# Two PSUM banks for the corrections u, and another order of the work, in a linear-attention and gated-convolution kernel on one core

## The chip, the core and the metric

The kernel runs on one core of a Trainium2 chip. The metric is the device time of one execution in microseconds; the time before is the median of three runs. Engines are named as in the profile: PE is TensorE (PEld its weight loads), DVE is VectorE, ACT is ScalarE, POOL is GpSimd, SP is SyncE, which issues most of the transfers.

## What is computed

Two parts, one after the other: a recurrent attention with decay and delta rule, whose output is the input of a network with a short convolution and a gate. B = 4, H = 8, S = 768 and D = 40; the network goes from 320 to 1024 features and back.

```
state = zeros((B, H, D, D))
for t in range(S):
    y[:, :, t] = einsum('bhd,bhde->bhe', rt, state)
    Sa = einsum('bhde,bhe->bhd', state, at)
    state = state * wt[:, :, None, :] - einsum('bhd,bhe->bhde', Sa, bt)
    state = state + einsum('bhd,bhe->bhde', vt, kt)
x = y.transpose(0, 2, 1, 3).reshape(B, S, H * D)
h = maximum(x @ w_in, 0)
conv = sum(conv_w[k] * shifted(h, k) for k in range(3))
out = (h * 1 / (1 + exp(-conv))) @ w_out
```

## The kernel before

The 768 tokens are cut into 24 steps of 32 tokens. Two steps are a pair (12 of them), prepared together; two steps of output are also a window of 64 tokens (12), the unit of the network.

For each pair, the loads w, a, k and b arrive by SP's queue; `decays` makes running products of the decays on VectorE, `decayed` multiplies them in and turns the results (products pa, pk and pb). `scores` makes the products ps for each step. `solve_in` and `solve` invert a small triangular system by 31 rounds of two operations (a multiplication, L566, and an addition, L572), on VectorE for even pairs and on GpSimd for odd ones, and bring the result `tt` into place through DRAM.

For each step, `chain` is the part that hangs on the step before: the products pp, from the state (L598) and from the values and scores (L608), are copied with a minus sign to `psb` by ScalarE; pu (L624) multiplies that by `tt` and gives u, the corrections; four evictions write u into `vu` beside the values (L631 to L638: ScalarE has the quadrants 1 and 2, VectorE 0 and 3); pn (L649) makes the state's addition from vu and the hatted keys kb; VectorE adds it, GpSimd scales the new state (L664). Beside the chain stand the turns of values, state and r (pv L673, pt, pr), the products pm (L717) and their masking ms, from_state (py L741), outputs (py L755), and `finish`, which turns the output (pq L776), scales it into xf (VectorE, L781) and splits it into xh and xl (ScalarE L789, GpSimd L791). `pack` copies parts of xh to xp and xl by three transfers on SP's queue. `moe_in` is the first projection, 16 products ph (L816) for each quarter of the features, of which the seventh reads xp, then the convolution, the gate and their evictions; `moe_out` is the second projection, po (L863).

The products ps, pm, pn, pp (two parts), pu and py (two parts) come as groups of 64 small products, of 32 or 40 columns each; the others are 3 to 16 larger ones. In what follows a run is a sequence of such small groups with no larger product between.

PSUM holds three tiles of two banks each (pp, pu, pn, ps and the others by `banks`) and two of one bank (ph and po). Though pu is a two-bank tile, its products use bank 0 alone.

The order is written out by hand. Each part of the work is a generator; the string ORDER names, one after another, which one advances to its next `yield` (`ch8*3`: the chain of step 8, three advances; we pieces of weights, ld lv lr loads, de decays, dd decayed, sc scores, si and so the solver, ch chain, vt st rt turns, fs from_state, pa pairs, ou outputs, fi finish, pk pack, mi and mo the two projections, mi3.1 being window 3 and quarter 1). `emit_all` (L926) walks it under `tc.manual_schedule()`, so each engine executes its instructions in the sequence in which this text emits them.

Of the kernel before, what the change touches and what calls it, by code (L numbers as in the profile page):

```python
# [38 lines left out]
we11 we10 dd2 ld3 dd2 we10*3 we12 so0 dd2*2 so0*2 we12 so0*2 so1 we11 we12*3 so1 sc4*3 sc5 we11
sc5*2 we11*2 so1 ro0 we13 we14 ro0*2 ch0*2 so1 we13*2 vt0 ch0 vt0*2 pa0 ch0 we15 we14*2 lv2*2 ch0*2  # L40
so1 ch1 we16 ch1 si2*2 pa0*2 we15*2 ch1 ou0 ch1 ou0*2 fi0 ch1 st1 so1 st1*2 fi0 ch1 we16*2 fi0 we17
vt1 we18 fs1*2 lv3*2 vt1*2 fi0*2 ch1 pa1 so1 rt1 pa1*2 ou1 lr2*2 rt1*2 ha3 ou1*2 ch1*2 fi1 ha3*2
we17*2 ha4 so1 ha4*2 ch2 we19 ch2 st2 ch2 fi1 so1*2 de3 we18*2 fi1 st2*2 fi1*2 fs2*2 we19*2 de3*2
dd3 we20 we21 pk0*2 mi0.3*2 we20*2 ld3*2 we22 ld4 ch2 we21*2 mi0.3 mi0.2*2 mi0.3 ch2 mi0.2 we22*2
ch2 mi0.2 mi0.3 mi0.2 ch2 dd3*2 vt2 ch2*2 mi0.2 dd3*2 lv4*2 dd3 mi0.3 dd3 ld4 vt2*2 dd3 mi0.2 so2
dd3*2 ch3 mi0.3 ch3 pa2 ch3 mi0.2*2 ch3 pa2*2 mi0.0*2 ch3 ld4 ou2 so2 ch3 ou2*2 fi2 vt3 ch3 mi0.0
fi2 lv5*2 ch3*2 so2 sc6 fi2 mi0.0 ch4 vt3*2 fi2*2 ch4 sc6*2 mi0.0 so2 sc7 ch4 st3 ha5 st3*2 sc7*2
ha5*2 fs3*2 so2 si3*2 pa3 st4*3 pa3*2 mi0.0 rt2 ou3 rt2*2 mi0.3*2 lr3*2 ha6 ou3*2 so2 mi0.0 fi3
mi0.1*2 ha6*2 mi0.1 fi3 de4 so2 fi3 fs4*2 ld4*2 mi0.1*2 fi3*2 pk1*2 so2 de4*2 dd4 so2*2 so3*2 dd4*2
mi0.0*2 mi1.0 mi1.2 dd4*4 so3 dd4 mi0.1 dd4*2 mi1.0*2 ch4 so3 mi1.0 mi0.1 ch4 mi0.1*2 mi1.1 mi1.0  # L50
ch4 ld5 mi1.0 mi1.1 vt4 ld5 mi1.1 ch4 so3 lv6*2 mi1.1 mo0.1 vt4*2 mi1.0 sc8 ld5 mi1.1 mi1.0*2 pa4
sc8*2 mi1.2 ch4*2 mi1.1 sc9 so3 mi1.2 sc9*2 mo0.1 pa4*2 si4*2 mi1.2 mi1.1 ch5 mi1.2 mi1.1*2 ou4
mi1.2 ch5 so3 ou4*2 fi4 ch5 st5 fi4 ch5 fi4 st5*2 mo0.1 ch5 fi4*2 mo0.1 so3 ch5 mo0.1*2 vt5 ch5
so3*2 so4 ha7 ch5*2 vt5*2 fs5*2 ha7*2 pa5 ch6*2 mi1.3*2 ch6 pa5*2 so4 ou5 st6 ou5*2 fi5 st6*2 rt3
fi5 lv7*2 so4 fi5 de5 rt3*2 fi5*2 ha8 ch6 ha8*2 ld5*2 de5*2 ch6 dd5 lr4*2 mi1.3 mo0.0 pk2*2 mi1.3
mi1.2 mo0.0 mi1.3 mo0.0 ld6 dd5*2 ch6 so4 dd5*2 vt6 ld6 mo0.0 ch6 lv8*2 dd5*2 ch6*2 dd5 fs6*2 vt6*2
# [957 lines left out]
```

## Time and profile before

| | before |
|---|---|
| median of three runs | 720.21 us (718.52 to 724.62) |
| profiled execution | 721.62 us |
| its span, first to last instruction | 719.9 us |
| mean granted clock of TensorE | 0.844 |
| PE, DVE, ACT, POOL busy | 579.1, 466.2, 251.9, 229.8 us |
| moved by DMA | 65.47 MB |

Times are in microseconds from the start of the span. In a timeline a row gives start, duration, engine, line, operation, output and inputs with their tile names, shapes, the number of instructions in the row, and in brackets how long the engine was idle before and what released it; "issue" means that nothing in the profile was waited for. The granted clock is a share of full speed.

### The profile page before, as it was taken

How to read it: one execution, taken by the hardware profiler on the slowest of the kernel's cores; microseconds unless marked ns; L12 is line 12 of the kernel's file. 1: busy time of each engine (PE TensorE's matmuls, PEld its weight loads, DVE VectorE, ACT ScalarE, POOL GpSimd, SP SyncE). 2: the span in 40 equal slices, each digit the busy share in tenths (PEclk: the TensorE clock that was granted, in tenths of full speed). 3: DMA queues.
4: the chain of work that ended last, by engine and by line, in shares of the span. 5: the costliest groups of instructions: out<-in, count | busy, mean ns of one | idle time of the engine just before them, and what ended most of it. 6: DMA issues, size and time to landing. Idle time of an engine off the chain costs nothing.

```text
span 719.9 us, 31917 instructions
## 1 busy us (share of the span) xinstructions
PE 579.1 (80%) x14265; PEld 498.3 (69%) x14265; DVE 466.2 (65%) x1091; ACT 251.9 (35%) x553; POOL 229.8 (32%) x466
## 2 busy tenths in 40 slices
PE   2760179668777988889888989989889899888998
PEld 2650168558766777677677778878778788777884
DVE  8888978878974765613866736987435686432541
ACT  1110013233242334323424435434433345543551
POOL 6010187001582010555014840124650108701000
PEclk9975557878898978967988989989988899997999
DMA  9889845552662643925724835634733534120011
GB/s 158 154 152 153 134 127 120 128 103 41 116 123 50 110 96 70 152 43 81 148 45 80 139 76 89 115 69 92 139 54 69 115 60 77 19 40 22 18 31 29
DMA packets 260278, 65.47 MB, mean 91 GB/s; under 512 B 233428, under 2 KB 255980, under 8 KB 260140
## 3 DMA queue, kind: packets, MB, share of 16 engines
q1 hardware_dynamic: 249940, 59.37, 46.3%
q10 hardware_dynamic: 10200, 4.06, 2.8%
q8 instruction: 112, 1.84, 1.1%
q14 instruction: 26, 0.21, 0.1%
HBM read 38.63 MB, written 10.22 MB: 68 GB/s over the span
## 4 chain that ended last, share of the span: by engine, by line
PE 26%; issue 6%; DMA 5%; DVE 5%; POOL 4%; ACT 2%; SPq 2%; ACTq 1%; POOLq 0%; DVEq 0%
PE po L863 7%; PE ph L816 5%; DMA bb<-bd 2%; PE pm L717 2%; POOL xx L572 2%; POOL st L566 2%; PE pv L673 1%; DMA bd<-at 1%; PE ps L510 1%; PE pn L649 1%; PE pp L608 1%; PE pt L700 1%; PE py L755 1%; PE pp L598 1%; PE pu L624 1%
## 5 line engine op out<-in xcount | busy, mean ns | idle before, releaser
L863 PE MATMUL po<-wo,g 128*128 128x320 f32 x384 | 120.5, 460 | 5.4 <-ACT hb L830 3.5
L845 DVE SCALAR_TENSOR_TENSOR cc<-hb,cw,cc 128x256 f32<-128x256 f32 x192 | 89.3, 527 | 21.5 <-ACT cc L837 21.4
L566 POOL TENSOR_TENSOR st<-xx,bb 128x126 f32<-128x126 f32 (+22 forms) x186 | 72.4, 389 | 75.8 <-DMA bb<-bd 30.8
L863 PEld LDWEIGHTS po<-wo,g 128*128 128x128 f32 x384 | 73.5, 201 | 31.8 <-issue 5.6
L572 POOL TENSOR_TENSOR xx<-xx,st 128x126 f32<-128x126 f32 (+22 forms) x186 | 77.6, 417 | 14.6
L664 POOL TENSOR_TENSOR state<-state,a 104x640 f32<-104x640 f32 x23 | 34.0, 1478 | 141.1 <-DVE state L661 125.4
L791 POOL TENSOR_TENSOR xl<-xf,xh 120x384 fp32r<-120x384 f32 x24 | 24.5, 1021 | 135.4 <-ACT xh L789 135.4
L566 DVE TENSOR_TENSOR st<-xx,bb 128x126 f32<-128x126 f32 (+22 forms) x186 | 55.8, 300 | 13.8 <-DMA bb<-bd 8.2
L816 PE MATMUL ph<-xh,wih 120*128 120x256 f32 x288 | 63.0, 331 | 0.0
L830 ACT ACTIVATE hb<-ph 128x512 f32<-128x512 f32 x48 | 28.7, 598 | 88.6 <-PE ph L816 88.3
L572 DVE TENSOR_TENSOR xx<-xx,st 128x126 f32<-128x126 f32 (+22 forms) x186 | 52.6, 283 | 6.4
L635 DVE COPY vu<-pu 32x320 f32<-32x320 f32 x48 | 23.3, 486 | 46.9 <-ACT vu L637 46.9
L855 DVE TENSOR_TENSOR g<-cc,hb 128x512 f32<-128x512 f32 x48 | 33.8, 714 | 25.1 <-ACT cc L850 20.7
L816 PEld LDWEIGHTS ph<-xh,wih 120*128 120x128 f32 x288 | 46.2, 210 | 3.4 <-issue 0.8
L510 PE MATMUL ps<-a,k 40*64 40x32 f32 x1536 | 36.0, 246 | 10.5 <-issue 5.3
L837 ACT ACTIVATE cc<-hb,cw 128x256 f32<-128x256 f32 x96 | 43.2, 500 | 0.2
L510 PEld LDWEIGHTS ps<-a,k 40*64 40x64 f32 x1536 | 32.7, 165 | 15.1 <-issue 9.0
L816 PE MATMUL ph<-xl,wih 120*128 120x256 f32 x192 | 41.8, 302 | 0.0
L724 DVE TENSOR_TENSOR ms<-pm,tri 128x512 f32<-128x512 f32 x24 | 16.5, 687 | 36.0 <-PE pm L717 35.9
L781 DVE TENSOR_TENSOR xf<-pq,pre 120x384 f32<-120x384 f32 x24 | 13.3, 554 | 39.7 <-PE pq L776 37.1
L717 PE MATMUL pm<-r,v 40*64 40x32 f32 x1536 | 34.0, 240 | 6.0 <-issue 4.9
L608 PE MATMUL pp<-vu,at 32*32 32x40 f32 x1536 | 25.9, 222 | 15.4 <-issue 15.4
(306 smaller groups left out, 1191.5 us busy)
## 6 DMA issues: line engine op xcount, KB each, us to landing
bb<-bd SPq DMA_DIRECT2D x24, 256.0 KB
w<-in_w_dram SPq DMA_DIRECT2D x24, 160.0 KB
a<-in_a_dram SPq DMA_DIRECT2D x24, 160.0 KB
k<-in_k_dram SPq DMA_DIRECT2D x24, 160.0 KB
rin<-in_r_dram SPq DMA_DIRECT2D x24, 160.0 KB
vu<-in_v_dram SPq DMA_DIRECT2D x96, 40.0 KB
b<-in_b_dram SPq DMA_DIRECT2D x24, 160.0 KB
k<-kt SPq DMA_DIRECT2D x24, 160.0 KB
```

Of the source, the lines that this page charges most:

```text
L510: nc.tensor.matmul(ps[half(z), x, y * 128 + hp * C : y * 128 + hp * C + C], k64[half(x, D), 2 * y + c, kp, z], a64[half(x, D), c, y, hp, z ...
L566: eng.tensor_tensor(t3, xx[:, 0:nj, i : i + 1].to_broadcast([128, nj, nt]), bb[:, i : i + 1, i + 1 :].to_broadcast([128, nj, nt]), ALU.mult,)
L572: eng.tensor_tensor(xx[:, 0:nj, i + 1 :], xx[:, 0:nj, i + 1 :], t3, ALU.add)
L608: nc.tensor.matmul(pp[quad(bi), x, hp * D : hp * D + D], at[kv(bi), c, y, x, hp], vu[kv(bi), y, KEY[x][hp], 0:D], start=(first and hp == 0 ...
L664: nc.gpsimd.tensor_tensor(new, new, al[..., 0:1].to_broadcast([SR, 2, 8, D]), ALU.mult)
L717: nc.tensor.matmul(pm[half(z), x, y * 128 + i * C : y * 128 + i * C + C], v64[half(x, D), y, i, half(z)], r64[half(x, D), y, i, quad(2 * z ...
L816: nc.tensor.matmul(ph[:, j], l[:, fs], x, start=(j == 0 and i == 0), stop=(i == len(passes) - 1), skip_group_check=True,)
L830: nc.scalar.activation(out=hb[:, :, :, 2 : W + 2], in_=ph, func=AF.Relu)
L837: nc.scalar.activation(out=cc[:, j], in_=hb[:, j, :, 1 : W + 1], func=AF.Copy, scale=cw[:, 1, f : f + 1],)
L845: nc.vector.scalar_tensor_tensor(out=cc[:, j], in0=hb[:, j, :, x : W + x], scalar=cw[:, x, f : f + 1], in1=cc[:, j], op0=ALU.mult, op1=ALU ...
L855: nc.vector.tensor_tensor(g, cc, hb[:, :, :, 1 : W + 1], ALU.mult)
L863: nc.tensor.matmul(po[:rows, :DM], parts(f), wo[:, f, :], start=(f == 0), stop=(f == NF - 1))
```

## The change

The products pu of odd batches are written to bank 1 of their tile instead of bank 0, the even ones stay in bank 0. The quadrants 1 and 2 hold the even batches and 0 and 3 the odd ones, so ScalarE's two evictions now read bank 0 and VectorE's two read bank 1. No instruction is added. The text of ORDER is replaced as a whole: the same steps of the same generators in another sequence. The diff, with the order cut to a few lines (the old text has a run around `ch8` and one around `ch11`, the new one around `ch1`; the new text's other lines are around step 8 and the scores 13 to 15):

```diff
--- before.py
+++ after.py
@@ -31,90 +31,93 @@
 )
 
 ORDER = """
...
-ch7 mi2.0 fi6 ch7*2 so4 vt7 mi2.0 fi6 sc10 lv9*2 vt7*2 fi6*2 so4 mi2.0 ch8 st7*2 ch8 sc10*2 so4*2
-mi2.0 ch8 sc11 fs7*2 sc11*2 mi2.0 pa7 mi1.3 rt4 pa7*2 mi1.3 mi2.0*2 mi2.1 rt4*2 ou7 mi1.3*2 mi2.1
...
-ch10*2 pa10 sc14 pa10*2 mi3.3 mi3.1*2 ch11 sc14*2 ch11 so6 sc15 ch11 mo2.1 sc15*2 ch11 so6 mo2.1*2
-ou10 ch11 st11 ou10*2 si7*2 mi4.1*2 st11*2 mi4.1 so6 fi10 ch11 mi4.1*2 vt11 ch11 lv13*2 vt11*2 fi10
...
+we0*4 ld0 de0*2 ld0 dd0*2 ld0 we1 we2 ld0*2 dd0 ld1 dd0*5 de0 de1 we1 dd0 de1 sc0*3 sc1*2 ld1 we2
...
+pa0*2 we11 st1 ha2 lr0 st1 we11 rt0 dd2 sc4*3 sc5 dd2 so1 sc5 we10 we11 lr1 we10 pa0 we12 lv1 we12
...
+fi7*2 ld6 de6 dd6 mo2.1 dd6 ha9 sc11 pk3 ch8*3 mo2.1 mo2.0 lr5 ou7 ch8 fs8 pa7 ch8 dd6*3 ld6 dd6*4
+lv0 mi3.0 vt8 si5 ch8 mi3.0 ch8 vt8 so5*2 mi3.0 fs8 mo2.0 so5 pa8*2 mi3.1*2 mi3.0*3 so5 mi3.1*2 ch8
+so5*4 ch8 lv9 mi3.1 ld7 mi2.3 mo2.1 mi3.1 de6 ou8 mi3.0 ld7 fi7 sc12*3 sc13*2 mi3.0 mo2.1 ou8
...
+mi4.2 sc13 lv9 mi4.1 mi4.3 mo3.0 dd7 pa11 so6*2 ou11*2 fi10*2 lr5 dd7 mi4.2 sc14 fi11 mi4.2 mi4.1
+fi11*2 mi4.2 mi4.3 sc14*2 mi4.3 rt5 ha12 fi11 mi4.1 mi4.3 ha12 sc15*2 mi4.3 rt6*2 sc15 ld8 st12
...
@@ -622,15 +625,16 @@
             x, hp = KAT[h]
             for bi in range(B):
                 nc.tensor.matmul(
-                    pu[bu(bi), 0, h * D : h * D + D], pd["tt"][quad(bi), c, 4 * x + hp],
+                    pu[bu(bi), bi % 2, h * D : h * D + D], pd["tt"][quad(bi), c, 4 * x + hp],
                     psb[quad(bi), x, hp],
                     start=(h == 0), stop=True, skip_group_check=True,
                 )
         yield
 
         for i, q in enumerate((1, 0, 2, 3)):
-            dst = vu[quad(q), int(q in (0, 3)), :, 0:D]
-            src = pu[quad(q), 0, 0:HD].rearrange("p (h d) -> p h d", d=D)
+            y = int(q in (0, 3))
+            dst = vu[quad(q), y, :, 0:D]
+            src = pu[quad(q), y, 0:HD].rearrange("p (h d) -> p h d", d=D)
             if i % 2:
                 nc.vector.tensor_copy(dst, src)
             else:
```

## Rows read from the trace of the kernel before

**Rows 1.** the page: busy times, and three groups on GpSimd

```profile
PE 579.1 (80%) x14265; PEld 498.3 (69%) x14265; DVE 466.2 (65%) x1091; ACT 251.9 (35%) x553; POOL 229.8 (32%) x466
...
L566 POOL TENSOR_TENSOR st<-xx,bb 128x126 f32<-128x126 f32 (+22 forms) x186 | 72.4, 389 | 75.8 <-DMA bb<-bd 30.8
...
L572 POOL TENSOR_TENSOR xx<-xx,st 128x126 f32<-128x126 f32 (+22 forms) x186 | 77.6, 417 | 14.6
L664 POOL TENSOR_TENSOR state<-state,a 104x640 f32<-104x640 f32 x23 | 34.0, 1478 | 141.1 <-DVE state L661 125.4
```

**Rows 2.** five stages: stretch, length, PE PEld DVE ACT POOL busy, PE clock, DMA share, GB/s

```profile
0.00:126.00 126.00, 61.49 (x1437) 54.16 (x1438) 106.10 (x269) 20.06 (x41) 48.75 (x103) 0.72 0.83 143
126.00:216.00 90.00, 67.18 (x1832) 59.34 (x1832) 74.33 (x175) 30.57 (x66) 31.23 (x67) 0.81 0.52 102
216.00:432.00 216.00, 186.25 (x5040) 161.63 (x5040) 126.33 (x286) 78.03 (x167) 72.90 (x151) 0.83 0.52 91
432.00:666.00 234.00, 213.12 (x5517) 184.33 (x5516) 138.13 (x315) 100.89 (x223) 75.96 (x145) 0.90 0.40 74
666.00:720.00 54.00, 51.01 (x444) 38.85 (x442) 21.32 (x47) 22.34 (x59) 1.00 (x1) 1.00 0.11 26
```

**Rows 3.** waits of VectorE up to 216 us: total, times, longest

```profile
DVE vu L635 <- ACT vu L637: 8.6, 10, 2.8
```

**Rows 4.** timeline, one step's evictions of u: start, duration, operation

```profile
446.97 0.42 ACT L637 COPY vu<-pu 32x320 f32<-32x320 f32 x1 [0.28 <-PE pu L624]
...
448.41 0.42 ACT L637 COPY vu<-pu 32x320 f32<-32x320 f32 x1 [1.02 <-DVE vu L635]
...
448.86 0.50 DVE L635 COPY vu<-pu 32x320 f32<-32x320 f32 x1 [0.48 <-ACT vu L637]
```

**Rows 5.** waits of TensorE after 110 us: total, times, longest

```profile
PE pp L608 <- issue: 15.4, 8, 2.5
PE ph L816 <- DMA xp<-xh: 8.4, 2, 5.6
...
PE pn L649 <- DVE vu L635: 2.2, 3, 1.3
...
PE pn L649 <- issue: 1.0, 2, 0.8
...
PE pn L649 <- ACT vu L637: 0.7, 2, 0.5
```

**Rows 6.** TensorE's timeline in three places

```profile
318.14 1.93 PE L510 MATMUL ps<-a,k 40*64 40x32 f32 x114
321.32 0.43 PE L510 MATMUL ps<-a,k 40*64 40x32 f32 x14 [1.25 <-issue]
...
366.53 0.43 PE L863 MATMUL po<-wo,g 128*128 128x320 f32 x1
366.89 1.14 PE L717 MATMUL pm<-r,v 40*64 40x32 f32 x64
...
372.36 0.22 PE L608 MATMUL pp<-vu,at 32*32 32x40 f32 x1 [1.94 <-issue]
...
582.54 2.33 PE L863 MATMUL po<-wo,g 128*128 128x320 f32 x8
```

**Rows 7.** two stretches around the gap at 370 us, columns as stages

```profile
370.50:373.90 3.40, 1.54 (x66) 1.42 (x67) 1.98 (x8) 0.44 (x1) 0.00 (x0) 1.00 0.02 5
373.90:377.40 3.50, 3.50 (x101) 2.30 (x102) 2.74 (x9) 0.80 (x2) 0.00 (x0) 0.51 0.03 7
```

**Rows 8.** TensorE's timeline, product pn at either level of the clock

```profile
101.31 1.83 PE L649 MATMUL pn<-vu,kb 64*64 64x40 f32 x62
...
449.73 1.13 PE L649 MATMUL pn<-vu,kb 64*64 64x40 f32 x64
```

**Rows 9.** timeline around the second window's copies

```profile
182.46 0.55 DVE L781 TENSOR_TENSOR xf<-pq,pre 120x384 f32<-120x384 f32 x1
...
188.86 0.36 PE L816 MATMUL ph<-xp,wil 120*128 120x256 f32 x1 [2.80 <-DMA xp<-xh]
```

More of the change, by code (lines that the diff above doesn't have):

```diff
@@ L39 @@
[L39 to L56, printed above, removed]
@@ new lines @@
+we14 mi0.0 ch3 we17 st3 ha5*2 fi2*2 ch3 mi0.0 we18 ou2 mi0.2 we4 vt3 we11 st3 we17 lv4 we5 so2 vt3
+dd3 pa2 de3 fi2 dd3 fs3*2 pa3 we18 pa3 fi2 we19 rt1 ch3*2 ch4 lr2 ch4 fi2 ch4*2 we20 mi0.1 mi0.3
+sc5 dd3 lv5 rt2 ou3*2 rt2 we19 sc6 mi0.0 we20 sc6 mi0.1 mi0.0 mi0.3*2 we15 ch4 mi0.0 fi3 mi0.3 sc6
+sc7 we21 lv1 ou3 mi0.3 mi0.2 sc7 fi3 mi0.3 fi3 mi0.2 ha5 ld3 ld4*2 fi3 ch4*2 we21 vt3 st4 mi0.2*3
+vt4 st4 ld4 mi0.3 ha6 we7 we22*2 pk1 si3 de4 ha6 mi0.2*2 mi0.3 ld4 lv2 vt4*2 we10 ch4 mi0.0 mi1.0
+mo0.0 dd3 mo0.0 de4 fi3 mi1.0*2 fs4 ld4 ha6 we12 we21 dd4*2 sc7 mo0.0 mo0.1 mo0.0 fs4 de4 pa3 mi0.2
@@ new lines @@
+mi1.0 ld5 pa4 mi1.0 si3 ch4 pa4 dd4 lr3 dd4*3 we17 dd4*2 ou4 ha7 so2 mi0.3 ha7 so3*2 ou4 mi1.0*3
+ou4 ch5 mi1.2 ch5 so3*2 ch5 mi1.2*3 we22 mi1.0 dd4 ch5 we20 mi1.2 st4 mi1.3 ro0 pa4 fi4 st5 lv6 ch5
+mi1.2*2 ch5 fi4 ch5 mi1.3 mi1.2 mi1.3 lr3 st5 we18 mo0.0 mi1.3*2 so3 ha7 so3 vt5 dd4 ld5 vt5 sc8*3
+sc9 mi0.1 we8 sc9 mi1.3 mi1.1*5 mi1.3 fs5*2 pa5*3 ld5 si4 mo0.1 fi4 mi1.2 ou5 de5 mi1.1 ch5 ou5 fi4
+mi1.3 ld5 fi4 fi5*4 de5 so3 ch5 ch6*2 pk2 we16 mi1.1 mo0.0 mo0.1*2 dd5*2 st5 dd5 mo0.1 mi1.1 mo0.1
@@ new lines @@
+mo1.1 dd5 so3 ld5 mi1.1 so3 st6 so3 dd5 mo1.1 mi2.0*3 so4 mo1.1 fi5 mi2.0 lr2 st6 ch6 mi2.1 ou5
+mi2.1 dd5 mi2.1 dd5 rt2 mo1.1 so4*2 rt3 mo1.0*2 mi2.1 vt5 mi2.1 ld6 rt3 fs6 dd5*2 mi2.0 ch6 mi2.2
+mi2.1 mi2.0 mi2.1 pk2 ch6 mi2.1 mo1.1 so4 mi2.2 lv7 fs6 vt6*2 we12 mi2.2 ch6 pa6 ch6 mi2.2 mi1.3
+pa6 so4 ch6 mi2.3 lr4 ou6*2 mi2.0 st6 so4*2 sc9 vt6 mi2.1 so4 mi2.2 mo1.0 st7 ch6 fi6 ch7*2 ld6 st7
+ch7 mo1.0 st7 ha8*3 sc10*2 ch7*2 mi2.0 rt3 fi6 ou6 mi2.3*2 vt7 mi2.2 fi6*3 mi2.3 lv5 sc10 vt7 sc11
+ch7*3 ld6 mi2.3 de5 lv8 mi2.2 ch7 mi2.0 mo1.1 sc11 lv8 so4 ha9*2 si4 mi2.3 pa6 si5 mi2.2 dd5
@@ new lines @@
+ha11 so5 mi3.2 so5 so6 mi3.2 vt9 mi3.2 mo2.0 st9 fs9 fi8*2 fs9 pa9 mi3.3 pa9 mo3.1 mo3.0 ch9 lv6
+ch9 ch10 ou9 ch10 mi3.0 so6*2 ou9 fi9 mo3.1 ch10 ld7 fi9 st10*2 de7 pk0 so6 ou9 fi9*2 ch10*2
+mo3.1*2 pk4 ch10 mi4.0*3 lv11 ld7 rt5 dd6 so6 ch10 mi4.0 rt5 mi4.0 de7 mi4.2 st10 pa9 mi4.2 dd7 lr6
+ld7 mo3.1 ch10 mi3.1 dd7 mi4.0 ch10 si6 pk1 dd7 ch11*2 vt10*3 ch11 mi4.2 ld8 lv12 so6 dd7*3 ch11
+dd7 mo3.0 mi4.1 fs10*2 dd7 pa10 ch11 pa10*2 ch11 mi4.0 st11*2 mo3.0 ou10 ha11 so6 de7 ou10 mi4.0*2
+ch11 so6 fi9 mo3.1 ou10 fs11 vt11*2 ld8 mi4.1 fi10 mi4.1*2 vt11 fs11 pa11 mi4.2 fi10 st11 fi10 ch11
@@ new lines @@
+ch13 mi5.3 ld9*2 dd8 mo4.0 mo4.1 mi5.0*2 ha14 st13 mi5.0 ha14*2 st13 sc16*3 sc17 ch13*2 ou12 vt13
+mo4.0 fs13*2 vt13 sc17 mi5.3 st13 pa13*2 mi5.3*2 ha15 so7 ha15*2 mi5.3 ou13*2 de9 fi13 si8 ld9 so7
+fi13 mi5.2*2 mi5.3 fi13*2 sc17 de9 dd9*2 ou13 mi5.2 rt7 mo4.0 lr6 pk6 so7 mi5.2*3 rt7 ch13 de9
+mo4.0 dd9 vt13 ch13 pa13 ha16*2 mi5.2 so7 so8 ch14 st14 fi13 st14 mi6.0 dd9*3 mi5.2 so8 ch14 mi5.2
+fs14 ch14 mi5.1 mi6.0 pk3 lv12 dd9 mi6.1 dd9 mi6.0 ch14 mi6.2 ch14 mi5.3 mi6.0 st14 vt14 mi6.0 fs14
+lv15 mi6.0 vt14 ch14 pa14 ch14 so8 pa14 ch14 mi6.2 si8 lv11 mo4.0 mi6.2 mo4.0 ch14 ch15*2 so8 ch15
@@ new lines @@
+st15 ch15*2 mo5.0 st15 ch15 ha16 ou14*3 mi5.3 mi6.0 vt14 ld9 ld10*3 vt15 mi6.2*2 fi14 mo5.0 so8
+ch15 so8 mo4.1 vt15 ch15 lr8 fi14 pa14 fi14*2 mi6.0 so8*2 mo5.0*2 fi14 fs15*2 pa15 dd9 pa15 sc18
+mi6.1*2 vt15 lv14 ch15 sc18*2 mi6.2 lr7 mi6.3 st15 ou15 sc19*2 mi6.2 ou15 mo5.1 fi15 mi6.2 de10
+lv16 lv17 mo5.0 ch16*2 pk4 mi6.2 ch16 dd9 mi6.3*2 sc19 fi15 de10 dd10 mo5.1 so8 ch16 fi15 pa15 ou15
+fi15 mi6.1*3 ch16 mi6.1 dd10 st16 mo5.1 st16 ha17 mo5.1 si9 dd10 ld10 mo5.1 so8 ha17 rt7 mi6.0 ch16
+rt8 vt16 mi6.3 pk7 ld10 mi6.3 lr8 ch16 ha17 mi6.3 rt8 vt16 dd10*2 si9 ch16 so9 mi6.1 vt16 dd10 st16
@@ new lines @@
+ch16 fs16 mi6.3 lv18 ch17*2 mi6.3 ld11 fi15 fs16 so9*2 dd10 mi6.1 mi7.0 ch17 mi7.1*3 mi7.0*3 so9
+dd10 so9 mo5.1 mi7.0 dd10 lr9 mo6.1 ch17*2 mi7.1 pa16 ch17 pa16 mi7.1*2 ch17 st17*2 mo6.1 mi7.0
+ou16*3 fs17 pa16 mi7.2 ld11 vt17 fs17 lv19 lv16 mi7.1*2 vt17 mi7.1 mi7.2 ld11 mi7.2 so9 de10 sc20*3
+sc21*2 si10*2 mi7.0 ch17 mi7.0 st17 mi7.0 mi6.3 mi7.2*3 so9 fi16 mo6.1 mi7.3*3 fi16*3 ha18 pa17*2
+so9 ha18 mi7.3*3 ha18 sc21 mo5.0 mo6.1*2 rt8 ou17 rt9 ou17 fi16 fi17 de11 fi17 rt9 fi17 de11 fi17
+mo6.0*2 pk8 dd10 so9 dd11 mo6.0*2 ha19 dd11*2 mi7.3 so9 ou17 so10 ha19 st18 mi7.2 ch17 mi7.3 lr9
@@ new lines @@
+mo6.0 ha19 ha20 ch18*2 so10 ld11 mo6.1 mi7.2 ch18 mi8.1 mi8.0 mi8.1 mi8.0*2 mi8.1 mo6.0 st18 ch18
+so10 ha20 mo7.1*2 ch18 ha20 dd11 mi7.2 so10 vt17 mi7.3 ch18 dd11 ch18*2 dd11*3 mo7.1 ch18 pk6 so10
+mi8.0 vt18 fs18 mi8.0 vt18 lv20 so10 pa17 ch19*3 dd11 st18 mo7.0 mo7.1 fs18 ch19*2 pa18 mo7.1 mo7.0
+ha21 pa18 ou18 ld11 so10 mi8.3 so10 mo7.1 mi8.0 ou18 st19*2 sc22 ch19 ou18 sc22*2 sc23 mi8.0 so10
+ch19 pk7 mi8.0 st19 mi8.1 sc23 mi8.1*2 lv19 mi8.3*2 so10 ch19 vt18 vt19 ha21 mi8.3 vt19 mi8.1*2
+mi8.3 mo7.0 mi8.2 ha21 ch19 ch20*2 si11 pk5 fi17 ch20 fi18 ch20 mi8.2 ch20 fi18 mi8.2 fi18 mi8.3
@@ new lines @@
+ch20 st20 mo7.0 fi18 mi8.2 lv21 ch20 lr10 ch20 rt9 pa18 fs19*2 pa19 vt19 mi8.2 mo7.0 st20 mi8.2
+pa19 sc23 mi8.2 so11 mi8.3*2 pa19 st20 fi18 mi8.2 mo8.1 vt20 mi8.2 lv22*2 ch20 ou19 ch21 ou19 ch21
+vt20 fi19 ha22 fi19 mi8.1 fi19 so11 ha22 vt20 ou19 ch21 mo7.0 mi8.3 ha22 mo8.1*2 rt10 mi8.0 rt10
+fi19 so11 mo8.1 ch21 fs20 so11 fs20 ch21 so11 pk9 mi9.1*3 ch21*2 pk8 pa20*2 mo8.1 mi9.1*2 mo8.0
+ch21 st21 mi9.1 rt10 dd11 mo8.1 st21 vt21 lr11 mi9.1*2 ou20*3 fs21 so11 fs21 pa20 mi9.2*2 vt21 st21
+lv23 fi19 fi20 mi9.2 fi20*2 pk9 pa21 mi9.0*2 fi20 mi9.2*2 pa21 so11 lv20 lv23 fi20 mi9.0 ou21*2
@@ new lines @@
+mi9.2 rt11 mi9.2*2 rt11 mi9.3 fi21*4 mi9.2 vt21 mi9.0 so11 mi9.0*5 ch21 mi9.3*2 mo8.0 ou21 mo8.0*2
+st22 ha23 mi9.3*2 lr11 ha23 mi9.1 pk10 mi10.0 so11 st22 mi9.3 fi21 mi10.0*3 lv17 mi9.3 mi10.0*2
+mi9.3 pa21 mi10.0 ch22 fs22 ch22*2 rt11 mo8.0*2 mi10.2 mi10.1*3 ch22 mi10.0 ch22 mi10.2*2 vt22 fs22
+pk10 ch22*2 vt22 lv18 mi10.2 ch22*2 mi9.3 mi10.1 mi10.0 mi10.3 mo9.0 ha23 mi10.2*2 pa22 ch23*2
+mi10.1 si11 mi10.2*2 ch23 mi10.3 pa22 mi10.1 mi10.3 mo9.0 ch23*2 st22 vt22 ou22*2 st23 mi10.2 fi22
+vt23 fi22 mi10.3 st23 mo9.0 pa22 mi10.1 vt23 ou22 fs23*2 pa23 so11 mi10.3*2 pa23 fi22 mo9.0 mo9.1
@@ L118 @@
+mo9.0 ou23 vt23 ou23 fi22 mo9.1 fi22 fi23*4 mi10.1*2 lv21 ch23 mo9.1 mi10.3*2 pk11 mo9.0 mo10.0
+mo9.1*3 mo10.0*2 ou23 pk11 mo10.0 mi11.0*5 mo10.0 mi11.2*3 mi11.0*2 mi11.2 mi11.0 mi11.2*2 mi11.1*3
+mo10.1 mi11.1 mo10.1 mi11.1 mi10.3 mi11.2 mi11.1*2 mi11.2 mi11.3*3 mi11.1 mo10.0 mi11.3*3 mo10.1*2
+lv13 mi11.3*2 en0 lr10 st23 de11 mi11.1 fi23 mo10.1*2 mo11.1*2 mo11.0 mo11.1*2 mi11.3 mo11.1
+mo11.0*4 en0 mo11.0 mi11.2 pa23 lv15 mo11.1 en0 mi11.0
 """
```

78 lines of the change are left out of this document (16 added, 62 removed).

## Prediction

> **What bounds the kernel now.** I read first the page's busy times [rows 1]: TensorE is busy 579.1 of 719.9 us, VectorE 466.2. Then I cut the span into five stages [rows 2]. Up to 216 us VectorE is busy 106.1 + 74.3 = 180.4 of 216 us while TensorE stands still for 64.5 + 22.8 us: this start, in which the weights are converted and the first pairs prepared, belongs to VectorE. From 216 us on TensorE is busy 450.4 of 504 us, so it is the bound there, and what lengthens the time is either idle time on it (29.8 + 20.9 + 3.0 us) or the granted clock (0.83, 0.90, 1.00). Next the waits of VectorE in the start [rows 3] and those of TensorE after 110 us [rows 5], to see what the idle time is. The reader is to see in rows 5 that the largest entries name no releaser ("issue"): ten rows of that view are of this kind, of which the first and the last are shown, and they sum to 40.8 us in 33 gaps; all other rows sum to about 33 us. So more than half of TensorE's idle time comes with all its inputs there. I then looked at where these gaps fall [rows 6] and at the clock around one [rows 7].
>
> **The gaps.** A group of 64 small products takes 0.77 to 1.2 us at the full clock. In rows 6 four groups follow each other from 366.89 us, and 1.94 us of nothing appear before the very last product of the fourth; in the other stretch, which begins with a group at 317.43 us, 1.25 us appear after another 114 products. Counted over TensorE's timeline after 110 us: 21 runs of three or more small groups hold 20 gaps, 67 shorter runs hold 6. Runs of exactly three have one in 4 of 5 cases, 1.10 us in the mean; gaps in shorter runs are 0.91 us in the mean; two more of about 2.0 us come before larger products, and the few that are left are below 0.3 us or lie beside a dependency. What the engine lacks in them the rows don't say. They say when it comes: here after 255 and 178 small products in a row.
>
> **The change, part by part.**
>
> *Two banks for u.* Nothing is added or removed: the same 64 products and four evictions a step, on other addresses. Before, the four evictions go in turns [rows 4]: from ScalarE's first at 446.97 to the end of VectorE's second, 448.86 + 0.50 = 449.36, are 2.4 us, and ScalarE's second waits 1.02 us for VectorE's first (which came late here, behind the solver). Without that delay four in a row are 0.42 + 0.47 + 0.42 + 0.50 = 1.8 us, with the steps between some 1.9. With one bank for each engine, two by two, it is about 0.47 + 0.50 = 1.0 us: 0.9 us less in each of 24 steps. Where is that on the path? TensorE waits for these evictions only a little: the two rows of the product pn sum to 2.2 + 0.7 = 2.9 us after 110 us [rows 5]. Larger work hides the rest; were the cover gone, the saving would be up to 24 x 0.9 = 21 us, all of which an order cut too close could need. In the start VectorE itself waits 8.6 us in ten waits for ScalarE's half [rows 3], and there VectorE is the bound. Some of these waits (the 2.8 us one) also contain the wait for u itself, so I take half: -4 us there, and -2 of the 2.9 us (bounds 0 and -12 together). The Trainium skill ("PSUM — Partial Sum Buffer", section "PSUM bank collisions raise a hardware error") says that two engines may use one bank at once as long as they are in different quadrants. These four evictions read different quadrants, and yet rows 4 show them in turn, so the turn-taking would be the program's own semaphores; if these stay, this term is 0 (rival D).
>
> *The order: fewer long runs.* Counted in the two texts of the order: runs of three or more small groups go from 23 to 18, runs of four or more from 15 (up to seven groups) to 2, runs of exactly three from 8 to 16. By the rates above, gaps after: in some 14 of the 18 runs (the others lie before 110 us or go without), 12 x 1.1 = 13.2 us; in 91 shorter runs, at 6 in 67, 8 x 0.91 = 7.3 us; before larger products 4.0 as now. That is 24.5 us instead of 40.8: **-16 us**. Bounds: 0, if the gaps go by the number of products, which is the same, and -30, if even runs of three now go without. I take the rate of the rows since length separates them so plainly (20 gaps in 21 runs, 6 in 67).
>
> *The clock.* Behind the gap of 1.94 us the granted clock goes from 1.00 to 0.51 [rows 7]: TensorE is at its upper level (2.4 GHz) through a stretch in which it worked 1.54 of 3.40 us, and at the lower (1.2 GHz) in the next, in which it worked all 3.50. At the lower level the same group of n takes 1.83 us for 62 products, at the upper 1.13 for 64 [rows 8], a factor of 1.67 for each product; I take 1.7. A mean clock of 0.81, 0.83 and 0.90 means that 0.38, 0.34 and 0.20 of these stages, 34 + 73 + 47 = 154 us, went by at the lower level. TensorE is busy in some 85% of it and would need 1/1.7 of that at the upper, so 154 x 0.85 x 0.41 = 54 us are lost. Spread over the 76.5 us of idle after 126 us (22.8 + 29.8 + 20.9 + 3.0) each us of idle costs 0.7 us more. 16 us less idle gives back 0.7 x 16 = **-11 us** (bounds 0, if other idle holds the clock down as well, and -21 with the 30 above).
>
> *More changes between small and large.* 93 runs become 109, and at their edges the pace suffers: one po holds 0.43 us before the small group at 366.89 us starts [rows 6], against 0.29 us for each of the eight in a row at 582.54 (2.33 / 8): 0.1 us, with the other edge of a run some 0.2. 16 x 0.2 = +3 us (bounds 0, +6). The Trainium skill ("TensorEngine Tiling (Array Packing)", section "Key Properties") says that a change of tiling mode drains TensorE, which speaks against a finer mixture; it names no price, and the rows give this small one.
>
> *What comes closer to its use.* VectorE's work ahead of the first projection into the gate network is about the same in both texts, so the start as a whole isn't shortened or lengthened. But the copies of a window (xp) get less room. From xf at 182.46 us, by ScalarE's and GpSimd's parts of it and three issues in turn on SP's queue, to the pass that reads xp at 188.86 are 6.4 us [rows 9]. In TensorE's work between a window's last turn and the pass that reads xp, before has 5.6 and 4.7 us in the first two windows, which wait 5.6 and 8.4 - 5.6 = 2.8 us [rows 5], and 8 to 37 in the ten others, which don't wait. So the need was 4.7 + 2.8 = 7.5 us in the second window and 11.2 in the first, where VectorE is the bound. After has 6.2 to 10 us in eleven of twelve, half of it at the edge of that need: 0 to 2 us each, and the first two wait less. In step 8, up to 16 pairs of the solver's products stand on GpSimd between the state's sum and its scaling (1.48 us), 16 x (0.389 + 0.417) = 13 us [rows 1], against 9.7 us of TensorE's work: some 3 us late. Five loads of v are issued at most 5 us of work ahead of use, instead of one; the queue of SP that issues them runs ahead of TensorE as a rule, so I count 0 to 2 us for each. Sum: idle 8.4 us of the two xp waits goes down by some 5, the new ones add some 8: +3 idle, with the clock 1.7 x 3 = +5 us (bounds 0 and +22, the latter with 2 us more in each of six windows).
>
> **Sum.** -16 - 11 - 6 + 3 + 5 = -25 us against the profiled execution of 721.6 us (a span of 719.9 and 1.7 around it): 696.6. It stood 1.4 us above the median of the runs, so the median after should be **695 us**.
>
> **The rivals.**
>
> *A, no change.* Gaps come by the number of small products and move to other places, the clock follows them. For it: the same products are issued, and 6 gaps did come in short runs. Against: 20 gaps in 21 long runs. Only the -6 of the banks and the +3 and +5 remain: 720.2 + 2 = 722; were half of the clock's term gained all the same, 717.
>
> *B, slower: the copies of a window come too late.* All twelve windows go through one SP queue, each behind the loads, solver transfers and outputs issued before. If that queue lags, the room of 6 to 10 us isn't enough for the 6.4 us, as it wasn't in the first two windows (5.6 and 2.8 us, mean 4.2). Ten more such waits are 42 us, with the clock 1.7 x 42 = 71. Against the 25 us of the sum the kernel is slower once the wait is above 25 / (12 x 1.7) = 1.2 us a window beyond what is counted; at 2.5 us it gives 695 + 51 = about 746. Against it: SP issues far ahead of TensorE in the later stages, where none of ten windows waits.
>
> *C, a stronger gain.* With no run of over three, the clock stays up throughout: gaps -30 and the clock's -21 instead of -16 and -11 give 695 - 24 = 671.
>
> *D, the banks bring nothing* since ScalarE and VectorE still go in turns: 695 + 6 = 701.
>
> **How the numbers follow.** My forecast 0.52 (its own range 680 to 712), D 0.06, C 0.09, A 0.19, B 0.14. About 1% is what a measurement of this kernel can tell from no change: 713 to 727.4 is the same. Faster 0.68 (forecast, C, D and 0.01 of A), same 0.18, slower 0.14. The range of 8 in 10 leaves out most of C below 674 and of B above 726: 674 to 726.
>
> **What would show it.** Right: TensorE's waits without a releaser go from 41 to about 25 us, those that stay lie in runs of three; the mean clock rises from 0.844 to about 0.88 or 0.90; ScalarE's and VectorE's evictions of u overlap and VectorE no longer waits for ScalarE at that line [rows 3]; the waits for xp are several and small. Wrong: the same 40 us of such waits (A); waits for xp or v over 20 us (B); evictions one after the other (D); a first stage that is longer by 10 us, since I held it as it was.

## The result and the profile after

The changed kernel takes **676.96 us** (671.27 to 678.28, four runs) against 720.02 us of the kernel before in the same comparison: a ratio of 0.938, with a 95% interval of 0.931 to 0.945. That is 43 us less, where 25 were forecast. It lies inside the range on record (674 to 726) and 3 us outside the likeliest case's own range (680 to 712). Below, the profiled executions are compared: 719.9 us before, 676.2 us after.

The page's busy times after, and its line for the queue that brings TensorE's instructions (number and size of the transfers), answer to [rows 1]:

```profile
PE 554.4 (82%) x14265; PEld 468.6 (69%) x14265; DVE 471.0 (70%) x1091; ACT 248.8 (37%) x553; POOL 227.9 (34%) x466
...
q8 instruction: 112, 1.84, 1.1%
```

TensorE executes the same 14265 products and is busy 24.7 us less; it stands still 676.2 - 554.4 = 121.8 us instead of 140.8. So 43.7 us are 19.0 us of idle time and 24.7 us of the same work done faster. VectorE's work is the same (471.0 against 466.2 us).

The stages after, columns as in [rows 2]:

```profile
0.00:126.00 126.00, 65.70 (x1442) 56.38 (x1444) 106.84 (x270) 19.37 (x38) 46.73 (x102) 0.65 0.71 125
126.00:216.00 90.00, 70.16 (x2025) 61.15 (x2012) 72.57 (x174) 34.61 (x76) 29.17 (x60) 0.89 0.68 125
216.00:432.00 216.00, 195.03 (x5368) 165.39 (x5367) 148.06 (x338) 89.31 (x200) 75.27 (x160) 0.94 0.55 103
432.00:666.00 234.00, 216.85 (x5429) 183.07 (x5430) 143.53 (x311) 104.71 (x239) 76.70 (x145) 0.94 0.37 68
```

The granted clock is what changed most: 0.81, 0.83 and 0.90 became 0.89, 0.94 and 0.94. Counted in the trace's clock records after 110 us, TensorE fell to its lower level (1.2 GHz) 24 times before, for 153.6 us in all, and 17 times after, for 73.6 us.

TensorE's waits after 110 us, columns as in [rows 5]:

```profile
PE pp L611 <- issue: 11.0, 7, 2.9
PE pu L627 <- issue: 5.6, 5, 1.8
PE pn L653 <- issue: 5.4, 4, 2.0
PE pn L653 <- DVE vu L639: 4.3, 5, 1.6
PE pv L677 <- ACT vu L641: 4.2, 5, 1.9
...
PE pz L532 <- DVE vu L639: 0.7, 1, 0.7
```

Three things are to be seen. The waits without a releaser are still there: ten rows sum to 33.6 us, against 40.8. The row of xp, 8.4 us before, is gone. And the three rows for the evictions of u, which summed to 3.2 us before (2.9 of them in [rows 5]), sum to 9.2 us. Why, the timeline of one step's evictions shows, the counterpart of [rows 4]:

```profile
431.89 0.42 ACT L641 COPY vu<-pu 32x320 f32<-32x320 f32 x1 [0.67 <-PE pu L627]
...
432.34 0.48 DVE L639 COPY vu<-pu 32x320 f32<-32x320 f32 x1 [2.86 <-ACT vu L641]
...
432.85 0.42 ACT L641 COPY vu<-pu 32x320 f32<-32x320 f32 x1 [0.54 <-DVE vu L639]
...
433.30 0.50 DVE L639 COPY vu<-pu 32x320 f32<-32x320 f32 x1 [0.48 <-ACT vu L641]
```

They go in turns as before, 1.91 us from the first start to the last end, though the two engines read different banks. VectorE's wait at that line in the first 216 us, 8.6 us in [rows 3], is now:

```profile
DVE vu L639 <- ACT vu L641: 11.3, 10, 5.2
```

### The profile page after: what moved, and what is told of

Read it like the earlier page. It is cut to its first block, busy times and chain, and to the rows that moved or that the text cites. A ratio compares the mean times of both kernels' runs of the same rounds, so it can differ in the third digit from the quotient of the medians.

```text
span 676.2 us, 31886 instructions
## 1 busy us (share of the span) xinstructions
PE 554.4 (82%) x14265; PEld 468.6 (69%) x14265; DVE 471.0 (70%) x1091; ACT 248.8 (37%) x553; POOL 227.9 (34%) x466
## 3 DMA queue, kind: packets, MB, share of 16 engines
q8 instruction: 112, 1.84, 1.1%
## 4 chain that ended last, share of the span: by engine, by line
PE 50%; DVE 23%; issue 10%; DMA 7%; ACT 3%; POOL 2%; SPq 2%; ACTq 1%; DVEq 0%; POOLq 0%
PE po L867 13%; PE ph L820 10%; PE ps L513 4%; DMA k<-kt 3%; DVE st L569 3%; DVE cc L849 3%; DVE xx L575 3%; PE pm L721 2%; PE pn L653 2%; PE py L759 2%; PE pv L677 2%; PE pu L627 2%; PE pp L611 2%; DVE vu L639 2%; ACT vu L641 2%
## 5 line engine op out<-in xcount | busy, mean ns | idle before, releaser
L867 PE MATMUL po<-wo,g 128*128 128x320 f32 x384 | 124.0, 462 | 2.0 <-DVE wo L288 1.5
L849 DVE SCALAR_TENSOR_TENSOR cc<-hb,cw,cc 128x256 f32<-128x256 f32 x192 | 96.2, 562 | 14.0 <-ACT cc L841 13.9
L867 PEld LDWEIGHTS po<-wo,g 128*128 128x128 f32 x384 | 72.0, 201 | 26.6 <-issue 4.4
L575 POOL TENSOR_TENSOR xx<-xx,st 128x126 f32<-128x126 f32 (+22 forms) x186 | 74.0, 398 | 14.6
L569 DVE TENSOR_TENSOR st<-xx,bb 128x126 f32<-128x126 f32 (+22 forms) x186 | 52.3, 281 | 8.9 <-POOL xl L795 1.5
L820 PEld LDWEIGHTS ph<-xh,wih 120*128 120x128 f32 x288 | 44.7, 205 | 3.4 <-ACT hb L834 0.2
L513 PE MATMUL ps<-a,k 40*64 40x32 f32 x1536 | 32.4, 237 | 17.0 <-DMA k<-kt 13.3
L513 PEld LDWEIGHTS ps<-a,k 40*64 40x64 f32 x1536 | 29.7, 155 | 20.0 <-issue 8.6
L627 PE MATMUL pu<-psb,tt 32*32 32x40 f32 x1536 | 24.1, 210 | 22.1 <-DVE wi22q L278 11.5
L611 PE MATMUL pp<-vu,at 32*32 32x40 f32 x1536 | 24.7, 213 | 21.0 <-issue 11.0
L653 PE MATMUL pn<-vu,kb 64*64 64x40 f32 (+1 forms) x1472 | 31.5, 232 | 10.2 <-issue 5.4
L627 PEld LDWEIGHTS pu<-psb,tt 32*32 32x32 f32 x1536 | 19.5, 115 | 29.1 <-issue 20.6
```

Of the source, the lines that this page charges most:

```text
L513: nc.tensor.matmul(ps[half(z), x, y * 128 + hp * C : y * 128 + hp * C + C], k64[half(x, D), 2 * y + c, kp, z], a64[half(x, D), c, y, hp, z ...
L569: eng.tensor_tensor(t3, xx[:, 0:nj, i : i + 1].to_broadcast([128, nj, nt]), bb[:, i : i + 1, i + 1 :].to_broadcast([128, nj, nt]), ALU.mult,)
L575: eng.tensor_tensor(xx[:, 0:nj, i + 1 :], xx[:, 0:nj, i + 1 :], t3, ALU.add)
L611: nc.tensor.matmul(pp[quad(bi), x, hp * D : hp * D + D], at[kv(bi), c, y, x, hp], vu[kv(bi), y, KEY[x][hp], 0:D], start=(first and hp == 0 ...
L627: nc.tensor.matmul(pu[bu(bi), bi % 2, h * D : h * D + D], pd["tt"][quad(bi), c, 4 * x + hp], psb[quad(bi), x, hp], start=(h == 0), stop=Tr ...
L653: nc.tensor.matmul(pn[half(x, m), z, (4 * y + hp) * D : (4 * y + hp) * D + D], kb[half(z), y, h * D : h * D + m], vu[half(z), y, h, 0:D], ...
```

## What the waits without a releaser are

In the kernel before, one long run holds three of them. TensorE's timeline there, start, duration, operation, count, and the wait in brackets:

```profile
303.50 0.62 PE L741 MATMUL py<-sd,r 40*32 40x40 f32 x46 [1.58 <-issue]
304.05 1.14 PE L717 MATMUL pm<-r,v 40*64 40x32 f32 x64
305.12 0.40 PE L624 MATMUL pu<-psb,tt 32*32 32x40 f32 x18
307.06 1.02 PE L624 MATMUL pu<-psb,tt 32*32 32x40 f32 x46 [1.54 <-issue]
308.00 1.29 PE L755 MATMUL py<-kb,ms 64*32 64x40 f32 x64
309.23 1.00 PE L649 MATMUL pn<-vu,kb 64*64 64x40 f32 x18
311.06 1.20 PE L649 MATMUL pn<-vu,kb 64*64 64x40 f32 x40 [0.83 <-issue]
```

The waits cut groups in the middle, and between one and the next lie 46 + 64 + 18 = 128 products, twice. With the products numbered through the whole program, the waits of the new kernel that are longer than 0.5 us stand after 110 us at

```
1482  2245  2373  2500  3008  3772  5047  5174  5553  6191  6827  7464  7718  8226  8989  9117  9499 ...
```

The differences are 127 or 128 or multiples of 127.3. Counting weight loads and the few semaphore instructions too, every such wait of either trace, but for one of the old, stands at the same place in a block of 256 instructions of TensorE (instruction 192 or 193 of 256). The page says what such a block may be: 1.84 MB came in 112 transfers on the instruction queue, 16.4 KB each (the page of before has the same line); 2 x 14265 instructions over 112 are 255. So the waits are read as standing where TensorE goes over to the next transfer's instructions: such a transfer landed 1.2 to 2.1 us, mostly 1.4, before each wait of the new kernel ended. One of them, in the stretch from 382.3 to 384 us, before the wait that ends at 385.44:

```profile
q8 instruction: 1, 0.02, 4.7%
```

From 303.50 to 307.06 and to 311.06 are 3.56 and 4.00 us. In none of the runs here did two such transfers land less than 3.2 us after each other (3.3 in the two traces). In groups without a pause at the upper clock a small product starts every 9 to 15 ns, so 128 of them are 1.2 to 1.9 us of work, and TensorE waits for the rest; a block with larger products takes longer anyway and shows nothing. It isn't a limit for each block: 19 of the 111 blocks in the trace of before took less than 3.5 us from border to border, the shortest 1.89 us, behind one of 13.6 us. An estimate can still be made with 3.7 us, a value between the intervals of the three waits. Adding up 3.7 us less the work of each block (other waits counted as work), where that is positive, gives a formula that can be worked out for borders at any place: by the old trace 44 us at the borders as they are (41 measured), and 41 to 50 wherever they are put; by the new trace 37 us as they are (34 measured), but from 20 to 44 depending on the place. This is the **theory of blocks**; the prediction's own is the **theory of runs**.

## The experiments

**The two halves of the change alone** (e1: the old ORDER with u in two banks; e2: the new ORDER with u in one, by this edit of the changed kernel)

```diff
-                    pu[bu(bi), bi % 2, h * D : h * D + D], ...
+                    pu[bu(bi), 0, h * D : h * D + D], ...
-            src = pu[quad(q), y, 0:HD]...
+            src = pu[quad(q), 0, 0:HD]...
```

> The old order of the work with u in two banks. The prediction's step (ScalarE and VectorE evict side by side): 6 us less than before, some 714 us, and VectorE's waits for ScalarE at the evictions of u fall from 46.9 us to below 10. The rival D (the program still makes the two engines take turns): 720 us, waits as before, evictions one after the other in the timeline.

> The new order with u in one bank as before. If the order carries all of the gain: 677 us. If the banks carry the 6 us of the prediction: 683 us.

Measured: e1 720.55 us, ratio 0.9997 (0.994 to 1.005); e2 677.45 us, ratio 0.942 (0.935 to 0.948). The order carries the whole gain, the banks nothing. VectorE's waits over the whole of e1:

```profile
DVE vu L636 <- ACT vu L638: 48.0, 41, 6.4
```

Those of the kernel before:

```profile
DVE vu L635 <- ACT vu L637: 46.9, 41, 6.3
```

The semaphores in the traces say the same: each eviction but the first waits for the one before it on the other engine, in both kernels.

**Moving the block borders** (e3, e4, e12 on the new kernel, e7 on the old one): in the scores of step 0 some products are executed again, which writes the same values and shifts all later instructions. EX is 32, 4 or 64; each is two products in the trace.

```diff
         ps = banks(f"ps{n}")
+        EX = 32 if n == 0 else 0
+        for e in range(EX):
+            y, hp, z, x = e // 16, e // 4 % 4, e // 2 % 2, e % 2
+            kp = KEKAT[KEY[x][hp]][1]
+            nc.tensor.matmul(...the product below, once more...)
```

> The changed kernel, with the first step's 32 score products executed twice (64 products in the trace, 128 instructions with their weight loads; same values written again). Theory of blocks, formed from the two traces: TensorE's waits without a releaser all lie at one place in each 256 of its instructions, which is one 16 KB transfer of its instruction queue, and a block of 256 whose work is shorter than some 3.7 us leaves TensorE waiting for the next one. From the changed kernel's trace the formula gives 37 us of such waits at today's place of the block borders and 22 us with the borders moved by 128 instructions: 15 us less idle and as much or a little less by the clock, 645 to 655 us, and the waits lie 64 products earlier in the sequence. Theory of runs, as in the prediction: the same runs, the same waits, 677 to 680 us.

> The changed kernel with only 4 score products of the first step executed twice (8 products in the trace, 16 instructions). Theory of blocks: the borders move by 16 instructions, for which the formula gives 43 us of waits instead of 37: 683 to 692 us. Theory of runs: 677 us.

> The changed kernel with the 32 score products of the first step executed three times, so with 64 products more: 128 in the trace, 256 instructions, one whole block. Theory of blocks: the borders lie again where they lay, between the same products, so the waits of the changed kernel come back (some 34 us) and the 15 us that 32 products gained are gone: 677 to 681 us. If 32 products gained by keeping TensorE busier early on, 64 gain as much or more: 662 us or less.

> The old kernel with the first step's 32 score products executed twice, the edit that was made to the new one. Theory of blocks: for the old order the formula gives 44 us of waits at today's borders and 46 with the borders moved by 128 instructions, so no gain: 720 to 725 us. If the extra products help for another reason (a busier TensorE in the start, a higher clock), it gains as the new order did, 705 us.

| run | borders moved by | formula, us | measured waits after 110 us | falls of the clock, us at the lower level | time, us | ratio to before |
|---|---|---|---|---|---|---|
| new | 0 | 37 | 33.6 | 17, 73.6 | 676.96 | 0.938 (0.931 to 0.945) |
| e4 | 16 | 43 | 35.7 | 14, 75.6 | 674.54 | 0.935 (0.926 to 0.945) |
| e3 | 128 | 22 | 22.5 | 9, 38.7 | 662.19 | 0.921 (0.914 to 0.929) |
| e12 | 256 | 37 | 39.1 | 15, 70.2 | 682.62 | 0.950 (0.939 to 0.961) |
| old | 0 | 44 | 40.8 | 24, 153.6 | 720.02 | 1 |
| e7 | 128 | 46 | 41.2 | 26, 152.8 | 714.61 | 0.989 (0.984 to 0.994) |

The kernel before took 720.0 to 727.6 us (medians) in the comparisons of this study, so kernels of different comparisons are best set side by side by their ratios. The pair e3 and e12 decides. 64 more products gain 15 us (e2, the new order with nothing added, took 677.45 us in the same comparison as e3); 128 more, one whole block, lose them again, and the waits are back between the same products. In the new kernel:

```profile
382.56 0.87 PE L653 MATMUL pn<-vu,kb 64*64 64x40 f32 x47
385.44 0.43 PE L653 MATMUL pn<-vu,kb 64*40 64x40 f32 x17 [2.01 <-issue]
```

In e12 (one block more), again 47 and 17:

```profile
387.16 0.88 PE L662 MATMUL pn<-vu,kb 64*64 64x40 f32 x47
390.56 0.43 PE L662 MATMUL pn<-vu,kb 64*40 64x40 f32 x17 [2.52 <-issue]
```

In e3 (half a block more) the same run of three groups goes through:

```profile
376.67 0.78 PE L754 MATMUL py<-sd,r 40*32 40x40 f32 x64
377.37 1.14 PE L730 MATMUL pm<-r,v 40*64 40x32 f32 x64
378.33 1.11 PE L662 MATMUL pn<-vu,kb 64*64 64x40 f32 x64
```

In e3, e4 and e12 every wait without a releaser after 110 us stands again at instruction 192 or 193 of its 256, the added ones counted. The theory of runs can't explain this: the runs are the same in all three. What the theory of blocks didn't hit is the size of e4 (43 us expected, 35.7 measured in the longest of its four executions, and no loss of time) and the full height of e3's gain (22 to 32 us expected, 15 measured): TensorE's idle time after 110 us went from 64.4 to 57.6 us only, as other waits grew from 26.1 to 30.4. In e7 the waits stayed as the formula says, while the time fell by about 1%, for which no wait accounts.

What an idle microsecond costs beside itself can be tried on the stretch after 110 us, the new kernel and then e3, in columns as in [rows 2]:

```profile
110.00:676.20 566.20, 501.76 (x13182) 423.87 (x13180) 376.58 (x856) 234.71 (x522) 183.39 (x366) 0.92 0.49 91
```

```profile
110.00:660.20 550.20, 492.56 (x13227) 415.80 (x13220) 378.70 (x861) 234.54 (x522) 189.99 (x372) 0.95 0.50 94
```

6.8 us less idle came with 9.2 us less busy time for 45 products more, and the clock went from 0.92 to 0.95: some 1.35 us for each in this pair, where the prediction took 0.7. It is no fixed price. In e12

```profile
110.00:680.60 570.60, 500.39 (x13249) 422.16 (x13247) 379.59 (x863) 235.25 (x523) 186.37 (x373) 0.94 0.49 90
```

TensorE stands still 5.8 us longer than in the new kernel (70.2 against 64.4), and yet the clock is higher and the busy time no longer.

**Start and rest** (e5: the new order until it has emitted 165 us of VectorE's work, then the old one without what is done; e6: the other way round)

```diff
-ORDER = """..."""   # one of the two orders
+ORDER = """..."""   # 390 (e5) or 414 (e6) advances of the one order, then the other's, less those already made
```

> The new order up to the step by which it has emitted 165 us of VectorE's work (about 190 us into the trace), then the old order with the steps already done left out. If the start and the rest gain each for itself: at 15% to 20% of TensorE's work the changed kernel is 10 to 12 us ahead, so some 709 us. If the start only does the same VectorE work in another sequence, as the prediction held: 720 us.

> The old order up to its step with 165 us of VectorE's work, then the new order. If start and rest add up: 677 + 10 = 687 us. If the gain is all in the rest: 677 us.

Measured: e5 716.82 us, ratio 1.002 (0.997 to 1.007); e6 695.01 us, ratio 0.965 (0.958 to 0.971). They don't add up as expected, and the reason is the seam. The time at which TensorE has done a share of its work (each product weighted with its time at the upper clock) is

| share of TensorE's work | old | e5 | new | e6 |
|---|---|---|---|---|
| 10% | 164.4 | 154.2 | 154.5 | 165.3 |
| 20% | 242.3 | 240.8 | 229.6 | 243.9 |
| 100% | 716.6 | 711.9 | 672.3 | 690.9 |
| from 20% on | 474.3 | 471.1 | 442.7 | 447.0 |

Up to 10%, e5 goes like the new order and e6 like the old; between 10 and 20%, where one order meets the other, e5 takes 86.6 us (old 77.9, new 75.1) and so loses what it had won. From 20% on e6 is as fast as the new kernel and e5 as slow as the old. So the rest's gain, 27 to 32 us, is the rest's own and doesn't need the new start. The start's 10 us are there at 10% in e5, and missing in e6, which ends 18 us behind the new kernel with 14 of them lost by 20%. Another seam moves the block borders too (e6 has 38.4 us of waits without a releaser after 110 us), and whether the new start would help another rest, e5 can't say.

**What the turns at the evictions cost** (e8: VectorE's two evictions read a constant, so that nothing is waited for, and u of the odd batches is left out; e9 to e11: all four on ScalarE, in the new kernel, there with e3's edit, and in the old kernel)

```diff
-                nc.vector.tensor_copy(dst, src)
+                nc.vector.tensor_copy(dst, sr2[quad(q), 0:HD]...)      # e8
```

```diff
-            if i % 2:
-                nc.vector.tensor_copy(dst, src)
-            else:
-                nc.scalar.copy(dst, src)
+            nc.scalar.copy(dst, src)                                   # e9, e10, e11
```

> The changed kernel, in which VectorE's two evictions of u in each step read a constant in SBUF instead of PSUM: the turn-taking of ScalarE and VectorE ends, and u of the odd batches is left out of the computation. It shows what evictions side by side would be worth. The changed kernel's TensorE waits 9.8 us in all for these evictions (products pn, pv and pz): if half of that goes and the clock gives as much again, 667 us. By the prediction's term for the banks (6 us): 671 us. If it is hidden by other work: 677 us.

> The changed kernel with all four evictions of u in a step on ScalarE, so that nothing is taken in turns: 4 x 0.42 = 1.7 us in a row instead of 1.9, and VectorE is rid of 48 copies, 23 us of work and its waits for ScalarE. If the price of the turns is what the run with a constant showed (about 14 us, most of it by VectorE and the clock): 663 to 668 us. If ScalarE's queue is now late for the network's evictions: 677 us or more.

> Both edits on the changed kernel: all four evictions on ScalarE, and the 32 score products of the first step executed twice. If the two gains are separate (15 us from the block borders, some 10 us from the evictions): about 650 us. If they are the same idle time seen twice: 660 us.

> The old kernel (old order, one bank) with all four evictions of u on ScalarE. If the turns cost the old order as much as the new one: 706 to 712 us. If they were hidden there, as TensorE's 2.9 us of waits for them after 110 us suggest, 716 to 720 us.

Measured: e8 662.57 us, ratio 0.917 (0.909 to 0.926), so 14 us below the changed kernel. There ScalarE's two copies follow each other and VectorE's lie ahead of them:

```profile
420.74 0.64 DVE L641 COPY vu<-sr 32x320 f32<-32x320 f32 x2
421.41 0.85 ACT L643 COPY vu<-pu 32x320 f32<-32x320 f32 x2 [0.43 <-PE pu L629]
```

TensorE's waits with a releaser after 110 us fall from 26.1 to 16.7 us, and the time at the lower clock from 73.6 to 44.7. That is an upper bound: VectorE's copies wait for nothing at all here, and take 0.35 us instead of 0.49. What ScalarE alone brings is less. e9 is 673.66 us, ratio 0.929 (0.923 to 0.936); e10 660.56 us, ratio 0.911 (0.904 to 0.919); e11 721.24 us, ratio 0.992 (0.987 to 0.997). Each is about 1% below its kernel without the edit, but only e11's interval keeps clear of that kernel's; for the new order it isn't settled. At the block borders these kernels wait more: the waits without a releaser after 110 us rose from 33.6 to 45.7 us in e9 (38.6 in e8), and from 40.8 to 47.7 in e11; in e10, with e3's borders, they are 22.9. e10 is the fastest kernel of the study that computes everything, 8.9% below the kernel before, and most of its lead over the changed kernel is the 32 products. Two separate tiles for the two banks, which might end the turns for good, were not tried.

## Why the prediction came out as it did

*Direction and mechanism.* Faster, through fewer waits without a releaser and a higher clock: that held. But of the terms of the sum that could be measured none held its size: the gaps and the banks gave less than forecast, the clock and the start more, and the copies saved time instead of costing it. These misses went against each other in part, and that the range still held the result, by 3 us, was luck in part. Of the 43.7 us, 24.7 came through the clock, where 11 were forecast.

*The gaps, -16 us.* This step failed. The rate "20 gaps in 21 long runs, 6 in 67 short ones" was a true count and the wrong rule: a long run holds more block borders and more blocks of small products alone. The waits went from 40.8 to 33.6 us, -7 and not -16. After 110 us 13 of the 15 runs of exactly three still had one, 16.6 us in all where the sum had 13.2 (with 12 of them, though its text speaks of 14 runs), and nine in shorter runs made 11.3 us where it had 7.3. e3 and e12 show that at equal runs the same waits can be 22 or 39 us. The row that could have told lay in the profile of before: the same 112 transfers of 16.4 KB, and gaps in the midst of a group, 128 products apart.

*The clock, -11 us.* The right mechanism, mis-sized by more than two. Idle time after 110 us fell by 12.9 us (77.3 to 64.4), the time at the lower level by 80 us; by the prediction's own conversion 80 x 0.85 x 0.41 = 28 us, and TensorE's busy time did fall by 24.7. The step that failed is the spreading of the loss evenly over idle time: falls lasted 6.4 us each before (153.6 / 24) and 4.3 after (73.6 / 17). What TensorE did in them differs. In the shortest falls, 7 of 24 before and 12 of 17 after, it worked without a pause until the clock rose, more than half of the time on larger products. In the 17 longer ones before it stood still for a part of their beginning, and in 9 of these it had small groups alone there. (Of the four longer ones after, three had such a pause and one, at 591.3 us, had none.) The beginning of a long fall before, in a run of seven small groups, and a short one after, in which po and pb follow, columns as in [rows 2]:

```profile
305.69:309.10 3.41, 2.04 (x110) 1.96 (x110) 0.73 (x2) 0.42 (x2) 1.32 (x4) 0.50 0.52 78
```

```profile
386.50:389.91 3.41, 3.41 (x12) 2.30 (x10) 2.81 (x7) 1.01 (x3) 2.99 (x2) 0.50 0.76 90
```

So shorter falls go with larger work behind a pause, which the new order brings sooner; that this is the cause no run shows by itself. The Trainium skill ("TensorE: Matmul & The Clock Gate", section "A second HAM failure mode: psum-queue depth-cycling") tells of a kernel in which TensorE pauses so often between groups of products that its clock swings between the two levels, and throughput is lost to the falling and recovering. The counts of falls agree, 9 in e3 with 22.5 us of waits and 15 in e12 with 39.1, though the pauses have another cause here.

*The banks, -6 us.* Rival D was right: e1 is 0.9997 of the kernel before. The mistake was to take the bank for the cause of the turns without asking what the semaphores are tied to; with the copies of VectorE off the tile pu the turns are gone (e8), with another bank of the same tile they aren't. So in this program they go with the tile. The term's size is not shown either: e8 bounds it at 14 us in the new order. The prediction's clause that an order cut too close could need what larger work now hides did come true, since TensorE's waits for these evictions rose from 3.2 to 9.2 us.

*What comes closer to its use, +5 us.* Wrong in sign. No wait for xp is left (-8.4 us). The need of 7.5 us and more was taken from the first two windows of before and was too high for the new order: there the pass of the second window comes 5.8 us after its xf (178.16 to 183.98), where [rows 9] have 6.4, and that of the last one 6.9 us (641.34 to 648.25), both without a wait. Step 8's GpSimd queue did not show: TensorE's waits for the state's scaling after 110 us sum to 1.0 us (3.3 before). One wait of 8.4 us in the first 110 us is put down to a load of v; in e2, with the same order, the wait before the same product is 9.3 us and put down to VectorE, so that the load was late isn't shown. The price of more changes between small and large, +3 us, was not measured by itself.

*The start, 0 us.* Wrong by 6 to 10 us for the start itself, though with the old rest behind it nothing of that was left in the end (e5). VectorE did as much in the first 126 us (106.8 against 106.1), but TensorE got further beside it: 10% of its work at 154.5 us instead of 164.4. VectorE is still the busier engine there; but an equal amount of its work did not mean an equal start. It may be that what VectorE does first decides what TensorE has to work on: by the text of the order 15 instead of 20 pieces of weights are two or more advances in ahead of the first projection. That this is the cause is argued, not shown.

*The rivals.* A (gaps by the number of products) was half right: nearly the same number of products gave 34, 22 and 39 us. B, late transfers, didn't happen. C overstated the gaps and understated the clock.

## What to carry to other kernels

Where TensorE stands still with all inputs there, look at how many instructions lie between such waits before looking at the work around them: a constant distance points to the fetching of instructions, and then the place of the block borders is a property of the whole program that any earlier instruction shifts. In this kernel it was blocks without larger work that waited, and a trial of some few dozen products more at the start is a cheap test that was worth 2% here. Before the clock is put into a sum, look at what follows each pause, for the pauses alone did not give its price here. Give two engines that evict side by side a tile each (not tried here), or give both halves to one engine, and look at the semaphores before a gain is counted.
